# Transposes of r and k in row tiles of 64 rows, and 48 instead of 64 weight columns in the small products of an RWKV-5 and tanh-shrink kernel

## The chip, the core and the metric

The kernel runs on one core of one Trainium2 chip. The metric is the device time of one execution in microseconds. Before the change it was 600.45 us, the median of three runs (600.21 to 601.79).

## The reference

Two blocks follow each other. The first is a linear recurrence with a state of 48 x 48 for each of 4 batches and 8 heads, over 768 steps. The second is a dense block with a nonlinearity, 3072 tokens, 384 to 2048 to 384:

```python
for t in range(S):                       # B, H, S, D = 4, 8, 768, 48
    cur = einsum('bhd,bhe->bhde', u * k[:, :, t], v[:, :, t])
    y[:, :, t] = einsum('bhd,bhde->bhe', r[:, :, t], state + cur)
    state = w[..., None] * state + einsum('bhd,bhe->bhde', k[:, :, t], v[:, :, t])
x = y.transpose(0, 2, 1, 3).reshape(B * S, H * D)
h = x @ w_in
out = (h - tanh(h)) @ w_out
```

All of it is in fp32.

## The kernel before

**Units.** The recurrence is computed in 24 units. A unit takes 64 steps (`SHORT`) of two batches: its tiles have 128 partitions, the halves z = 0 and 1 being the two batches, and hold 8 heads of 48 values, each padded to 64 (`PAD`); the pads of r, of the decayed k (`kw`), of v and of the states are zero. Unit n is chunk `ch = n // 2` of batch pair `n % 2`. Heads come in four pairs p, with i = 0 and 1 in a pair.

**Steps of a unit**, in the function `unit` (from line 723):

- `fetch` (line 747) loads r, k and v with two DMAs each on SP's queue.
- `turn` (line 762) transposes r, and then k or `kw`, on TensorE: four transposes of 128 x 128, one for each pair of heads, so that heads lie on partitions and the 2 x 64 steps on columns. r goes into one PSUM bank of a two-bank tile and k into the other. This tile is `x_banks` for the first 16 units and `yk_ps` for the last 8 (`two`).
- `scale_r` (line 766) multiplies r by the powers of the decay on DVE into `rT`; `scale_k` (DVE, first two units) or `copy_k` (ACT, line 775) brings k into `kT`.
- `from_state` (line 808) multiplies the state by `rT` into `y_ps`, 16 small products. `levels` (line 819) makes the 64 x 64 blocks of k times r; DVE copies what lies above the diagonal into `at` (line 918), and ACT writes the diagonal (line 789) from the sums of r k u.
- `outputs` (line 831) adds v times `at` to `y_ps`, and `to_state` (line 845) makes the new part of the state in `kv_ps`; both are 16 products, which the trace shows as 32 instructions, as each is issued in two parts. All small products go through `put` (line 718) as tiles of 64 x 64 of the array, four of them apart in rows and columns. `to_state` is made for 22 units; the last chunk needs none.
- `to_xt` and `to_rest` (ACT, lines 864 and 869) copy `y_ps` into the dense block's input, POOL's queue moves the remaining rows (`fill`, line 874), and `keep` (line 879) adds the new part to the state.

**Dense block.** Class `Dense`: `h` (line 168) multiplies by w_in, ACT makes the tanh and helping terms, DVE joins them, and `o` (line 206) multiplies by w_out. From the ninth of 16 column blocks on and for the last token blocks the second product uses seven products in place of eight (`products`, line 257). Weights arrive as 64-bit floats and are converted on DVE and ACT (lines 137 to 143), up to about 210 us.

**What sets the order.** Nothing runs in the order of the source. `add` gives each step its engine, a planned cost, the steps that it follows and, for TensorE, the number of instructions. `Plan.order` (line 450) simulates all engines' queues with these costs and searches for a good order with some 3000 random tries; the result is each engine's fixed order. Where it leaves TensorE idle in the opening part it places filling products (line 654). Any change of a cost or a number of steps in lines 889 to 932 can so move every queue.

Of the kernel before, what the change touches and what calls it, by code (L numbers as in the profile page):

```python
# [11 lines left out]
F32 = mybir.dt.float32  # L12
# [4 lines left out]
ALU = mybir.AluOpType  # L17
# [14 lines left out]
C = 128  # L32
PAD = 64
# [267 lines left out]
class Plan:  # L301
# [214 lines left out]
def near(ctx, tc, r, k, v, w, u, out, shared, moe_w_in, moe_w_out):  # L516
# [12 lines left out]
    ps_a = ctx.enter_context(tc.tile_pool(name="n_ps_a", bufs=1, space=PSUM))  # L529
# [12 lines left out]
    HALF = [slice(z * SHORT, (z + 1) * SHORT) for z in range(2)]  # L542


    rows = fixed("rows", [2 * NP, 2, PAD])
    V.memset(rows, 1.0)
    same = fixed("same", [128, SHORT])
# [3 lines left out]
    V.memset(by[:, :, 0:1], 0.0)  # L551
    V.memset(plus, 0.0)
    V.memset(plus[:, :, 0:1], 1.0)

    def padded(name, count, new=fixed):

# [20 lines left out]
    before = before.bitcast(I32)[:, None, None, :].to_broadcast([128, 2, NP, SHORT])  # L577


    yk_ps = ps_a.tile([128, 2, 512], F32, name="yk_ps", tag="yk_ps")  # L580
    banks_now = [ExitStack(), ExitStack()]

    def banks(at, name, shapes):
# [34 lines left out]
    y_ps = yk_ps[:, :, :256].rearrange("e z (p t) -> e z p t", p=NP)  # L618
    kv_ps = yk_ps[:, :, 256 : 256 + NP * D].rearrange("d z (p e) -> d z p e", p=NP)
# [6 lines left out]
    w_up = fixed("w_up", [128, NP, 2, SHORT])  # L626
# [25 lines left out]
    def fills(to):  # L652
        def run(n):
# [6 lines left out]
    now = [add(e, 1.25 if e == "ACT" else .87, lambda e=e, at=at, x=x: e_of[e].dma_start(out=rows[at : at + NP, :, :D], in_=x.rearrange("(p i) d -> p i d", i=2)), due=-1, data=.05)  # L660
           for e, at, x in (("SP", 0, w), ("ACT", NP, u))]
# [16 lines left out]
    now = add("POOL", 1.0, bounds, [keeps])  # L678
    now = add("PE", .2, lambda: T.matmul(tab[0:1, 0:1], ok[:, 0, :1], shared["one"], start=True, stop=True), [now, downs])
# [20 lines left out]
    for n in range(weights.count):  # L700
# [14 lines left out]
    def flat4(t):  # L715
        return t.rearrange("d p z t -> d (p z t)")

    def put(*args, **how):
        T.matmul(*args, skip_group_check=True, **how)  # L719

# [2 lines left out]
    def unit(n):  # L723
# [3 lines left out]
        ch, half = divmod(n, 2)  # L727
        j, slot = divmod(n, L)
        steps_at = slice(ch * SHORT, (ch + 1) * SHORT)
        t = SimpleNamespace(at=ats[n % 2])  # L730
        rt, vt, kw, state = rts[n % (AHEAD + 1)], vts[n % (AHEAD + 1)], kws[n % 2], states[half]
        two = n >= L * (FIRST + 2)
        pair = yk_ps if two else x_banks[n == 1]
        sign = -1.0 if slot and j in dense.negative else 1.0
        r_ps, k_ps = (pair[:, i] for i in range(2))
        lev, own_lev = (pair[:, :, at : at + 256].rearrange("s i (p t) -> s i p t", p=NP) for at in ((256, 0) if two else (0, 256)))
        none = SimpleNamespace(**{x: None for x in "r k v turn rT kw kT rk du own diag state lev cp out xt rest add decay".split()})
        b1, b2, b3 = (units[n - i] if n >= i else none for i in (1, 2, 3))
# [22 lines left out]

        def turn(src, to):
            for p in range(NP):
                T.transpose(to[:, p * C : (p + 1) * C], src[:, 2 * p : 2 * p + 2, :].rearrange("t h d -> t (h d)"), ident)  # L764

        def scale_r():
            t.rT = work.tile([128, NP, 2, SHORT], F32, name="rT", tag="rT")
            V.tensor_tensor(flat4(t.rT), r_ps, flat4(w_up), ALU.mult)  # L768

        def scale_k():  # L770
            t.kT = work.tile([128, NP, 2, SHORT], F32, name="kT", tag="kT")
            V.tensor_tensor(t.kT, k_ps.rearrange("d (p z t) -> d p z t", p=NP, z=2),
                            inverse[:, :, None, 1:].to_broadcast([128, NP, 2, SHORT]), ALU.mult)

        def copy_k():
            t.kT = work.tile([128, NP, 2, SHORT], F32, name="kT", tag="kT")
            A.copy(flat4(t.kT), k_ps)

        def own():
            t.rk = work.tile([128, H, D], F32, name="rk", tag="rk")  # L780
# [18 lines left out]
                    for i in range(2):  # L799
                        put(own_lev[HALF[z], i, p], t.kU[HEAD[i], p, z], t.rT[HEAD[i], p, z], start=True, stop=True)  # L800

        def to(i, z):


            i = i ^ z if swap else i
            return slice(i * PAD, (i + 1) * PAD)

        def from_state():
            for p in range(NP if ch else 0):
                for z in range(2):  # L810
                    for i in range(2):
                        put(y_ps[to(i, z), z, p], state[HEAD[i], z, p], t.rT[HEAD[i], p, z],
                            start=p == 0, stop=False)

        def between():
# [13 lines left out]
            G.tensor_copy(extra[slot][:, :, :, D:], vt[:, 2 * NK :, :D].rearrange("s i (k x) -> s i k x", k=NK))  # L829

        def outputs():
            for p in range(NP - direct):
                for i in range(2):
                    for z in range(2):
                        put(y_ps[to(i, z), z, p], vt[HALF[z], 2 * p + i], t.at[HALF[z], i, p],
                            start=p == 0 and not ch, stop=p == NP - 1)
            for p in range(NK if direct else 0):
                for i in range(2):
                    for z in range(2):
                        put(y_ps[to(i, z), z, p], extra[slot][HALF[z], i, p], t.at[HALF[z], i, NK],  # L840
                            start=False, stop=p == NK - 1)
            if not direct:
                to_state()

        def to_state():
            for p in range(NP if more else 0):
                for i in range(2):
                    for z in range(2):
                        put(kv_ps[i * PAD : (i + 1) * PAD, z, p], kw[HALF[z], 2 * p + i], vt[HALF[z], 2 * p + i, :D],
                            start=p == 0 or not two, stop=True)  # L850

        def given(out, y):
# [36 lines left out]
        free = [b1.cp, b1.diag] if n > 2 else [units[0].cp, units[0].diag] if n == 2 else []  # L889
        if two:  # L890
            free = [b1.xt, b1.rest, b1.add, b1.cp, b1.diag]
        x.turn = add("PE", .46, lambda: turn(rt, r_ps), [x.r] + free, steps=8)
        x.kw = add("DVE", .47, lambda: V.tensor_tensor(kw[:, :, :D], t.kt[:, :, :D], w_down, ALU.mult), [x.k, downs, b2.out])
        x.turn_k = x.rk = add("PE", .46, lambda: turn(t.kt if direct else kw, k_ps), [x.k if direct else x.kw] + free, steps=8)
        both = [x.turn, x.turn_k]
        x.rT = add("DVE", .62, scale_r, both + [ups])
        if direct:
# [4 lines left out]
        if product:  # L902
            now = add("ACT", 1.05, own_k, [x.kT, w_us])
            x.own = add("PE", .7, own_levels, [now, x.rT, b2.out], steps=64)
            x.diag = add("DVE", .64, lambda: V.copy_predicated(t.at, same.bitcast(I32)[:, None, None, :].to_broadcast([128, 2, NP, SHORT]), own_lev), [x.own, b2.out])
        else:
            x.rk = add("DVE", .47, own, [x.r, x.k, b2.du, b1.rk if not b1.own else None])
            now = add("DVE", .47, lambda: V.tensor_tensor(t.rk, t.rk, ub, ALU.mult), [x.rk, bonus])
# [9 lines left out]
        x.cp = add("DVE", .64, lambda: V.copy_predicated(t.at, before, lev), [x.lev, b2.out] + ([] if product else [x.diag]))  # L918
# [105 lines left out]
    now, done = 22.0, 0  # L1024
# [335 lines left out]
```

## Time and profile before

| what | value |
|---|---|
| median of three runs | 600.45 us (600.21 to 601.79) |
| the profiled execution | 599.5 us |
| its span | 597.7 us |
| granted TensorE clock | 0.999 |
| TensorE products (PE), busy | 579.0 us, 5589 instructions |
| TensorE weight loads (PEld), busy | 491.5 us, 5589 instructions |
| DVE, ACT, POOL, busy | 465.6, 403.0, 203.7 us |
| transposes of r and k, line 764 | 29.6 us busy, 192 instructions |
| small products, line 719 | 63.6 us busy, 3008 instructions |
| DMA | 33.77 MB, 53 GB/s of HBM over the span |

The table is from the page of the profile, the rows of lines 764 and 719 from the groups by line and form. PE is a product and PEld the load of its stationary side; a load can lie under the product before it. A product's row lasts until its last result is written, and the next begins before that, so that busy times of products overlap and the distance from start to start is the cost of one. "Idle before" is the time for which an engine did nothing ahead of an instruction, and the name after the arrow is what ended it. A tile's name in a row stands for all its buffers: x_ps and yk_ps are the PSUM tiles for r and k, lev, y and the new states.

### The profile page before, as it was taken

To read this page: it belongs to the slowest core of one execution; us is meant where nothing else is said; L and a number is where in the kernel's file an instruction comes from. 1 tells how busy PE (TensorE), PEld (TensorE's weight loads), DVE (VectorE), ACT (ScalarE), POOL (GpSimd) and SP (SyncE) were. 2 spreads that over 40 slices of the span, in tenths; PEclk is the share of its full clock that TensorE was granted. 3 is DMA by queue.
4 is the path that set the end of the run, shared out by engine and by line. 5 is a ranking of instruction groups with operands and counts; after the bars stand their busy time and mean duration, and the time that the engine had idled before them with its cause. 6 is when DMAs were issued, how large, how long until landed. Compare 5 with 4: busy or idle time off the path is not lost.

```text
span 597.7 us, 14262 instructions
## 1 busy us (share of the span) xinstructions
PE 579.0 (97%) x5589; PEld 491.5 (82%) x5589; DVE 465.6 (78%) x781; ACT 403.0 (67%) x902; POOL 203.7 (34%) x366
## 2 busy tenths in 40 slices
PE   8879999999999999999999999999999999999996
PEld 5557677777777779899999999989889888999995
DVE  5799979999999999986777775665776775555765
ACT  3798798899668867766555563765675866556552
POOL 5002212201000324454555463442435354334620
PEclk9999999999999999999999999999999999999999
DMA  6976986935211311201110011120211200100101
GB/s 127 228 132 121 168 195 110 142 94 114 60 53 27 62 29 24 50 5 24 28 26 13 16 28 34 34 47 15 55 22 27 42 1 9 27 2 7 27 3 31
DMA packets 86325, 33.77 MB, mean 56 GB/s; under 512 B 78536, under 2 KB 80680, under 8 KB 86248
## 3 DMA queue, kind: packets, MB, share of 16 engines
q1 hardware_dynamic: 81084, 25.57, 22.0%
q0 software_dynamic: 4992, 6.99, 5.5%
q8 instruction: 46, 0.75, 0.6%
q14 instruction: 31, 0.25, 0.1%
q10 hardware_dynamic: 172, 0.20, 0.1%
HBM read 26.94 MB, written 4.72 MB: 53 GB/s over the span
## 4 chain that ended last, share of the span: by engine, by line
PE 72%; DVE 14%; ACT 5%; issue 4%; DMA 3%; SPq 2%; DVEq 0%; POOL 0%; ACTq 0%; POOLq 0%
PE h L168 34%; PE p L257 25%; PE o L206 5%; PE yk_ps L719 5%; SPq L752 2%; DVE tg L196 2%; DVE tg L194 1%; DVE g L192 1%; DVE g L198 1%; DMA vt<-in_v_dram 1%; PE yk_ps L764 1%; ACT at L789 1%; DMA kt<-in_k_dram 1%; DVE rT L768 1%; DVE mixed L266 1%
## 5 line engine op out<-in xcount | busy, mean ns | idle before, releaser
L168 PE MATMUL h<-xt,w_in_sb 128*128 128x256 f32 x1152 | 281.1, 381 | 1.9 <-DVE w_in_sb L143 0.9
L168 PEld LDWEIGHTS h<-xt,w_in_sb 128*128 128x128 f32 x1152 | 212.5, 190 | 32.7 <-DVE g L192 1.4
L242 POOL TENSOR_TENSOR sg<-g 128x256 f32<-128x256 f32 x69 | 53.1, 770 | 171.4 <-DVE g L198 105.3
L194 DVE SCALAR_TENSOR_TENSOR tg<-s,tg 128x512 f32<-128x512 f32 x96 | 69.5, 723 | 53.5 <-ACT tg L181 28.6
L257 PE MATMUL p<-mixed,sg 128*128 128x192 f32 x426 | 104.0, 326 | 0.0
L181 ACT ACTIVATE tg<-h 128x512 f32<-128x512 f32 x96 | 57.2, 596 | 55.7 <-PE h L168 55.7
L192 DVE TENSOR_TENSOR g<-h,th 128x512 f32<-128x512 f32 x96 | 66.0, 688 | 26.8 <-ACT tg L181 10.6
L177 ACT ACTIVATE s<-h 128x512 f32<-128x512 f32 x96 | 57.4, 598 | 41.4 <-PE h L168 41.3
L876 POOL DMA_DIRECT2D xt<-rest x66 | 32.3, 495 | 142.7 <-ACT rest L855 142.7
L179 ACT ACTIVATE th<-h 128x512 f32<-128x512 f32 x96 | 57.4, 598 | 33.4 <-PE h L168 33.2
L198 DVE COPY_PREDICATED g<-small,tg 128x512 f32<-128x512 int32 x96 | 75.6, 787 | 4.0
L196 DVE SCALAR_TENSOR_TENSOR tg<-q,tg 128x512 f32<-128x512 f32 x96 | 68.2, 711 | 9.8 <-ACT q L183 7.4
L257 PEld LDWEIGHTS p<-mixed,sg 128*128 128x128 f32 x426 | 75.0, 190 | 0.0
L206 PE MATMUL o<-w_out_sb,g 128*128 128x384 f32 x192 | 69.8, 490 | 1.7 <-DVE g L198 1.6
L257 PE MATMUL p<-w_out_sb,g 128*128 128x192 f32 x284 | 71.2, 332 | 0.0
L183 ACT ACTIVATE q<-s,m1b 128x512 f32<-128x512 f32 x96 | 69.7, 726 | 0.7
L185 ACT ACTIVATE small<-s,smallb 128x512 f32<-128x512 f32 x96 | 69.4, 723 | 0.3
L257 PEld LDWEIGHTS p<-w_out_sb,g 128*128 128x128 f32 x284 | 51.8, 190 | 7.1 <-DVE o L285 0.2
L789 ACT ACTIVATE at<-same,du 128x64 f32<-128x64 f32 x184 | 47.7, 342 | 5.3 <-DVE du L785 5.0
L206 PEld LDWEIGHTS o<-w_out_sb,g 128*128 128x128 f32 x192 | 35.5, 190 | 18.4 <-issue 1.9
L244 POOL TENSOR_TENSOR sg<-sg,g 128x128 f32<-128x128 f32 x69 | 43.2, 626 | 5.1
L246 POOL TENSOR_TENSOR sg<-sg,g 128x128 f32<-128x128 f32 x69 | 36.9, 534 | 5.1
(132 smaller groups left out, 688.2 us busy)
## 6 DMA issues: line engine op xcount, KB each, us to landing
st<-in_moe_w_out_dram SPq DMA_DIRECT2D x8, 768.0 KB, 5.0
rt<-in_r_dram SPq DMA_DIRECT2D x48, 96.0 KB, 2.9
vt<-in_v_dram SPq DMA_DIRECT2D x48, 96.0 KB, 3.5
st<-in_moe_w_in_dram SPq DMA_DIRECT2D x16, 288.0 KB, 5.4
kt<-in_k_dram SPq DMA_DIRECT2D x44, 96.0 KB, 3.4
out_dram<-o POOLq DMA_DIRECT2D x44, 96.0 KB, 2.1
st<-in_moe_w_in_dram POOLq DMA_DIRECT2D x16, 96.0 KB, 4.8
xt<-rest POOLq DMA_DIRECT2D x66, 16.0 KB, 2.2
```

Source lines behind the costliest of these rows:

```text
L168: self.nc.tensor.matmul(t.h2[:, z], self.w_in_sb[:, t.f // 2, kk, z * 128 : (z + 1) * 128], self.xts[t.j][:, kk].rearrange("p b t -> p (b ...
L177: A.activation(out, t.h, AF.Square)
L179: A.activation(out, t.h, AF.Tanh)
L181: A.activation(out, t.h, AF.Tanh, scale=G1)
L183: A.activation(out, t.s, AF.Square, bias=self.m1b)
L185: A.activation(out, t.s, AF.Relu, bias=self.smallb, scale=-1.0)
L192: V.tensor_tensor(t.g, t.h, t.th, ALU.subtract)
L194: V.scalar_tensor_tensor(t.tg, t.s, C4, t.tg, ALU.mult, ALU.mult)
L196: V.scalar_tensor_tensor(t.tg, t.q, K1, t.tg, ALU.add, ALU.mult)
L198: V.copy_predicated(t.g, t.small.bitcast(I32), t.tg)
L206: self.nc.tensor.matmul(self.outs[i], t.g2[:, z, i * C : (i + 1) * C], self.w_out_sb[:, t.f + z, :], start=t.first and z == 0, stop=t.last ...
L257: self.nc.tensor.matmul(ps[bank][:, half * n : (half + 1) * n], a, b, start=t.first and half == 0, stop=t.last, skip_group_check=True)
```

## The change

`turn` makes eight transposes in place of four: each takes the 64 rows of one half z and 128 columns, against a 64 x 64 corner of the identity, and writes 64 columns. Half 0 goes to the first PSUM bank and half 1 to the second, both for r (columns 0 to 255) and for k (columns 256 to 511). The three readers follow with another index order. In `from_state`, `outputs` (not for the first two units) and `to_state` the stationary side has 48 columns in place of 64, so that 48 partitions are written and not 64. Since `y_ps` is read in all its partitions, `yk_ps` is set to zero once at the start, on DVE. The planned costs and numbers of instructions are changed, and with them the searched order. The core of the diff:

```diff
+    V.memset(yk_ps, 0.0)
...
-        r_ps, k_ps = (pair[:, i] for i in range(2))
+        r_ps, k_ps = (pair[:, :, at : at + 256].rearrange("d z (p t) -> d z p t", p=NP) for at in (0, 256))
...
         def turn(src, to):
             for p in range(NP):
-                T.transpose(to[:, p * C : (p + 1) * C], src[:, 2 * p : 2 * p + 2, :].rearrange("t h d -> t (h d)"), ident)
+                for z in range(2):
+                    T.transpose(to[:, z, p], src[HALF[z], 2 * p : 2 * p + 2, :].rearrange("t h d -> t (h d)"), ident[HALF[z], HALF[z]])
...
-            V.tensor_tensor(flat4(t.rT), r_ps, flat4(w_up), ALU.mult)
+            V.tensor_tensor(t.rT, r_ps.rearrange("d z p t -> d p z t"), w_up, ALU.mult)
...
-            A.copy(flat4(t.kT), k_ps)
+            A.copy(t.kT, k_ps.rearrange("d z p t -> d p z t"))
...
-        def to(i, z):
+        def to(i, z, n=PAD):
...
-            return slice(i * PAD, (i + 1) * PAD)
+            return slice(i * PAD, i * PAD + n)
...
-                        put(y_ps[to(i, z), z, p], state[HEAD[i], z, p], t.rT[HEAD[i], p, z],
+                        put(y_ps[to(i, z, D), z, p], state[HEAD[i], z, p, :D], t.rT[HEAD[i], p, z],
...
-                        put(y_ps[to(i, z), z, p], vt[HALF[z], 2 * p + i], t.at[HALF[z], i, p],
+                        put(y_ps[to(i, z, n), z, p], vt[HALF[z], 2 * p + i, :n], t.at[HALF[z], i, p],
...
-                        put(kv_ps[i * PAD : (i + 1) * PAD, z, p], kw[HALF[z], 2 * p + i], vt[HALF[z], 2 * p + i, :D],
+                        put(kv_ps[HEAD[i], z, p], kw[HALF[z], 2 * p + i, :D], vt[HALF[z], 2 * p + i, :D],
...
-        x.turn = add("PE", .46, lambda: turn(rt, r_ps), [x.r] + free, steps=8)
+        turns, turned = .46, 16
+        x.turn = add("PE", turns, lambda: turn(rt, r_ps), [x.r] + free, steps=turned)
...
-            now = add("PE", .68, from_state, both + [x.rT, b1.xt, b1.rest, b1.add, b2.decay, x.kT], steps=64)
+            now = add("PE", .66, from_state, both + [x.rT, b1.xt, b1.rest, b1.add, b2.decay, x.kT], steps=64)
...
-        x.lev = add("PE", .7 if two else (1.35 if swap else 1.75) if ch else .7, levels,
+        x.lev = add("PE", .7 if two else (1.33 if swap else 1.73) if ch else .7, levels,
...
-        x.out = now = add("PE", .95 if direct else 1.3, outputs,
+        x.out = now = add("PE", .95 if direct else 1.21, outputs,
...
-            now = x.out = add("PE", .6, to_state, [now, x.kw], steps=64)
+            now = x.out = add("PE", .55, to_state, [now, x.kw], steps=64)
```

More of the change, by code (lines that the diff above doesn't have):

```diff
@@ L542, in near @@
     HALF = [slice(z * SHORT, (z + 1) * SHORT) for z in range(2)]
+    yk_ps = ps_a.tile([128, 2, 512], F32, name="yk_ps", tag="yk_ps")
     rows = fixed("rows", [2 * NP, 2, PAD])
@@ L577, in near @@
     before = before.bitcast(I32)[:, None, None, :].to_broadcast([128, 2, NP, SHORT])
-    yk_ps = ps_a.tile([128, 2, 512], F32, name="yk_ps", tag="yk_ps")
     banks_now = [ExitStack(), ExitStack()]
@@ L712, in near @@
         converted += now
-    def flat4(t):
-        return t.rearrange("d p z t -> d (p z t)")
     def put(*args, **how):
@@ L763, in turn @@
             for p in range(NP):
-                T.transpose(to[:, p * C : (p + 1) * C], src[:, 2 * p : 2 * p + 2, :].rearrange("t h d -> t (h d)"), ident)
+                for z in range(2):
+                    T.transpose(to[:, z, p], src[HALF[z], 2 * p : 2 * p + 2, :].rearrange("t h d -> t (h d)"), ident[HALF[z], HALF[z]])
         def scale_r():
             t.rT = work.tile([128, NP, 2, SHORT], F32, name="rT", tag="rT")
-            V.tensor_tensor(flat4(t.rT), r_ps, flat4(w_up), ALU.mult)
+            V.tensor_tensor(t.rT, r_ps.rearrange("d z p t -> d p z t"), w_up, ALU.mult)
         def scale_k():
             t.kT = work.tile([128, NP, 2, SHORT], F32, name="kT", tag="kT")
-            V.tensor_tensor(t.kT, k_ps.rearrange("d (p z t) -> d p z t", p=NP, z=2),
+            V.tensor_tensor(t.kT, k_ps.rearrange("d z p t -> d p z t"),
                             inverse[:, :, None, 1:].to_broadcast([128, NP, 2, SHORT]), ALU.mult)
@@ L831, in outputs @@
         def outputs():
+            n = PAD if direct else D
             for p in range(NP - direct):
@@ L891, in unit @@
             free = [b1.xt, b1.rest, b1.add, b1.cp, b1.diag]
-        x.turn = add("PE", .46, lambda: turn(rt, r_ps), [x.r] + free, steps=8)
+        turns, turned = .46, 16
+        x.turn = add("PE", turns, lambda: turn(rt, r_ps), [x.r] + free, steps=turned)
         x.kw = add("DVE", .47, lambda: V.tensor_tensor(kw[:, :, :D], t.kt[:, :, :D], w_down, ALU.mult), [x.k, downs, b2.out])
-        x.turn_k = x.rk = add("PE", .46, lambda: turn(t.kt if direct else kw, k_ps), [x.k if direct else x.kw] + free, steps=8)
+        x.turn_k = x.rk = add("PE", turns, lambda: turn(t.kt if direct else kw, k_ps), [x.k if direct else x.kw] + free, steps=turned)
         both = [x.turn, x.turn_k]
```

## The prediction

> **What bounds the kernel now.** I read the page's busy shares first, then the busy time of each engine by stretch, and then the order of TensorE's work around one unit of the recurrence.
>
> ```profile
> PE 579.0 (97%) x5589; PEld 491.5 (82%) x5589; DVE 465.6 (78%) x781; ACT 403.0 (67%) x902; POOL 203.7 (34%) x366
> ```
>
> TensorE is busy 97% of the span. By stretch (columns: stretch, its length, then busy us of PE, PEld, DVE, ACT, POOL):
>
> ```profile
> 0.00:106.00 106.00, 95.60 (x1778) 68.88 (x1782) 88.93 (x162) 80.96 (x229) 24.23 (x67) 1.00 0.82 155
> 106.00:225.00 119.00, 116.88 (x991) 87.56 (x986) 117.06 (x190) 95.62 (x195) 15.33 (x27) 1.00 0.34 71
> 225.00:355.00 130.00, 129.09 (x717) 119.98 (x708) 103.53 (x175) 80.97 (x160) 67.90 (x108) 1.00 0.11 24
> 355.00:537.00 182.00, 181.38 (x1842) 163.95 (x1841) 118.03 (x193) 112.53 (x259) 75.59 (x130) 1.00 0.13 26
> ```
>
> From 106 us on TensorE runs without a break, so there any microsecond of its work is a microsecond of the span. Before 106 us it has gaps, DVE and the DMAs (share 0.82) are as full, and the chain of waits over 0 to 106 us gives the small products (line 719, tile yk_ps) 8.5% and the transposes (line 764, tile x_ps) 3.5%: 12.7 us of that stretch. By then TensorE has spent about 47 us on all that is not dense work (my sum by the prices below), so a microsecond saved there is worth about a quarter (12.7/47).
>
> The prices come from TensorE's order of work (start, length, instructions; a group's true cost is from its start to the next start, since the ends overlap):
>
> ```profile
> 181.88 0.60 PE L764 MATMUL x_ps<-ident,kw 128*128 128x128 f32 x4
> 182.41 0.69 PE L719 MATMUL yk_ps<-at,vt 64*64 64x64 f32 x32
> 182.93 0.63 PE L719 MATMUL yk_ps<-vt,kw 64*64 64x48 f32 x32
> 183.49 1.56 PE L206 MATMUL o<-w_out_sb,g 128*128 128x384 f32 x4
> 184.88 1.46 PE L168 MATMUL h<-xt,w_in_sb 128*128 128x256 f32 x6
> 186.18 0.60 PE L764 MATMUL x_ps<-ident,rt 128*128 128x128 f32 x4
> 186.62 1.46 PE L168 MATMUL h<-xt,w_in_sb 128*128 128x256 f32 x6
> 187.91 1.45 PE L206 MATMUL o<-w_out_sb,g 128*128 128x384 f32 x4
> 189.30 0.69 PE L719 MATMUL yk_ps<-rT,state 48*64 48x64 f32 x32
> ```
>
> A turn (four transposes) between dense products takes 186.18 to 186.62, 0.44 us: 4 x 0.109, no boundary cost. Ahead of 64x64 products it takes 0.53: 0.09 is lost between the two shapes. The four o products take 1.29 elsewhere, but 1.39 when 64x64 products follow (187.91 to 189.30) and again 1.39 just after them (183.49 to 184.88). There the wait is doubled: in the single records the last small product starts 0.149 before the first o product, 0.058 of it its own turn, 0.091 idle, and then 0.104 of the next start is an unhidden weight load. So a change of array shape costs 0.09 us, and 0.055 (a transpose's load) to 0.104 (a dense load) more.
>
> **What the Trainium skill says.** "TensorEngine Tiling (Array Packing)", Key Properties: changing the tiling mode drains TensorE, and different tiles load weights and multiply in parallel. The trace agrees on both: 0.09 us at each change above, and line 719's four tiles start 7 ns apart with a new set of four each 58 ns. The same page, Gotcha 1: row tiles must not write one PSUM bank together; the change does put the halves into two banks. "TensorE: Matmul & The Clock Gate", LDWEIGHTS: a load costs its columns over 1.2 GHz, whatever the rows. The trace agrees for ordinary loads, not for transposes:
>
> ```profile
> L168 PEld LDWEIGHTS h<-xt,w_in_sb 128*128 128x128 f32 x1152 | 212.5, 190 | 32.7 <-DVE g L192 1.4 <-PE x_ps L764 1.1 <-PE x_ps L719 0.3
> L719 PEld LDWEIGHTS yk_ps<-rT,state 48*64 48x64 f32 x704 | 12.3, 134 | 12.4 <-DVE state L882 5.7 <-issue 2.7 <-DVE rT L768 1.5
> L764 PEld LDWEIGHTS x_ps<-ident,rt 128*128 128x128 f32 x64 | 7.4, 142 | 3.9 <-DVE at L918 1.8 <-issue 1.2
> ```
>
> 128 columns take 56 ns longer than 64 (190 against 134), but a transpose's 128 columns load in 142; two of line 649's loads start 61 ns apart. "PSUM — Partial Sum Buffer", bank collisions: two engines must not use one bank at once. After the change both r and k lie in both banks, so the DVE that scales r and the ACT that copies k can't overlap. They do not now either (columns: waits in all us, times, longest):
>
> ```profile
> ACT kT L777 <- DVE rT L768: 5.2, 6, 2.3
> DVE rT L768 <- ACT kT L777: 2.0, 5, 0.9
> ```
>
> **The change part by part.**
>
> (1) Transposes, inside. 48 turns of 4 x 0.109 = 0.436 become 4 pairs of 64-row tiles. If a pair runs side by side, its period is the longer of a transpose load (0.061 by line 649) and 64 moving columns (0.058, line 719); I take 0.058, 0.233 a turn. 48 x (0.233 - 0.436) = -9.7 us. Upper bound: pairs that don't overlap, or that lose the fast load, 0.109 to 0.122 a pair, 0.44 to 0.49 a turn: +9.8 to +12.3 on this term.
>
> (2) Transposes, boundaries. The 64x128 shape is new, so every edge to dense work now changes shape. In the changed program's order the 48 turns form 39 runs: 27 follow dense work, 12 small products; 37 are followed by dense work, 2 by small products. Cost: 27 x (0.091 + 0.055) + 37 x (0.091 + 0.104) + 2 x 0.091 + 12 x 0.055 = 3.9 + 7.2 + 0.2 + 0.7 = 12.0 us. The old order pays 5 x 0.093 (turn to products) and 12 x 0.055 = 1.1, and 2 more exits from small products to dense (0.2). Net +10.7. A turn alone between dense work thus goes from 0.44 to about 0.58; two back to back fall from 0.87 to 0.83. No row of before shows an edge between 128x128 and 64x128 at full clock; the lower bound is no drain, 64 x 0.091 = 5.8 us less. I take the drain, for the reason above.
>
> (3) New states (line 849). Both sides are now 48 columns. The order shows a set of four at 58 ns where 64 columns load and, once, at 45 ns where the load was already done and 48 move. 8 sets x 0.0134 = 0.107; 22 units have this step: -2.35 us. Lower gain: none, if the load has a floor of 64.
>
> (4) Outputs and reads of the state. Weights have 48 columns, but 64 still move, so the period stays 58 ns; only the first two loads, exposed, are shorter: 2 x 0.013. 22 + 22 groups: about -1.1, at least 0.
>
> (5) Evacuations. rT (0.69 us) and kT (0.58) now read two banks with a four-index pattern. Line 772 already reads with one and takes 0.69 as line 768 does; I take zero (bound +0.06 each, 2.9 us over 48, on DVE and ACT, felt only before 225 us).
>
> (6) The memset of yk_ps on DVE. 1024 columns by the row "plus" (260 columns, 0.28) is 1.1 us, from 2.15 to about 3.3; DVE is idle until 5.74 and the first product into that tile starts at 5.23, so it is hidden. Without that cover it costs 1.1.
>
> (7) Instruction stream: 192 transposes and loads more, 384 on 11,178, some 1.6 of the 46 packets of the instruction queue. Taken as zero; a fetch that TensorE waits for costs up to 2 us each.
>
> (8) Plan. The order is searched anew with changed costs, so all queues are rearranged, SP's loads and POOL's stores among them. My own sum of TensorE's work before is 565.1 us in a span of 597.7: 32.6 idle, some 20 of it before 106 us. One tenth of this more or less is 3 us.
>
> Sum over all: -9.7 + 10.7 - 2.35 - 1.1 = -2.4 us of TensorE work. Split at the output step of the twelfth unit (105.7 us): -3.0 before it, where turns lie in pairs or by small products; +0.5 after it, where most turns stand alone in dense work. On the span: 0.25 x -3.0 + 0.5 = -0.25. The profiled execution took 599.5 us with span 597.7 (1.8 outside); the median is 600.45, 0.95 above it. Carried to the median: 600.2.
>
> **Rivals.** *A, forecast: 600.2, no measurable change* (about 0.3%, 1.8 us, is what a measurement of this kernel can tell), own range 598.7 to 602.2. *B, the early saving counts in full*: 600.45 + 0.5 - 3.0 = 598.0, and lower if edges of the row shape don't drain (-5.8) or the plan is luckier. For it: TensorE is busy 90% before 106 us. Against: DVE and DMA are as full and the chain is theirs. *C, the new plan wastes a tenth more idle time*: 603.5. For it: DVE is at 98% from 106 to 225 us, so a later DVE step has no slack. *D, the pairs of row tiles don't run side by side*: place, line 764; price 0.49 a turn instead of 0.23; it decides for slower once a pair costs over about 0.074 (0.016 x (88 pairs + 104 x 0.4) = 2.1 us). The late 22 turns lose 22 x 0.25 = 5.5 in full, the early 26 lose 6.5 at a quarter to the half: 600.2 + 5.5 + 2.4 = 608. Against it: line 719's row tiles do overlap now, and the fast load stood in the one 8-row transpose (177 ns at the slow opening clock, 187 for a 128-row one). That the change does nothing is excluded: a quarter of the states' columns leaves the program.
>
> **How the numbers follow.** A 0.40, B 0.25, C 0.20, D 0.15. Faster by over 0.3% is B, 0.25; within 0.3% is A, 0.40; slower is C and D, 0.35. The range takes in C and most of B and D: 596.5 to 608.5.
>
> **What would show it.** Right: transposes of 64 rows starting 7 ns apart and sets 58 ns apart, a lone turn at 0.58, o after it at about 1.39; yk_ps<-vt,kw at 0.45 instead of 0.56 to the next start; TensorE's work about 2 us less. Wrong: single transposes 60 ns apart or more (D), a dense group after a turn at 1.29 (no drain, B), or more idle on TensorE ahead of 225 us (C).

## The result, and the profile after

The changed kernel takes 606.27 us (median of six runs, 605.43 to 608.19) beside 600.76 for the kernel before on the same chip (600.21 to 601.82): ratio 1.0093, 95% interval 1.0074 to 1.0112. It is 5.5 us slower. The profiled execution took 607.26 us, its span 605.5. From the page of the kernel after: busy shares, the clock that TensorE was granted in 40 slices (9 is full), and the instruction queue.

```profile
PE 582.4 (96%) x5781; PEld 485.7 (80%) x5781; DVE 466.4 (77%) x782; ACT 403.3 (67%) x902; POOL 201.0 (33%) x366
...
PEclk9889899999999999999999999999999999999999
...
q8 instruction: 47, 0.77, 0.5%
```

The clock was below full speed in three of the first five slices, up to 76 us; before, all 40 digits were 9. By stretch (length, busy us of PE, PEld, DVE, ACT, POOL, then granted clock, DMA share, GB/s):

```profile
0.00:106.00 106.00, 91.53 (x1696) 62.84 (x1697) 86.91 (x155) 75.79 (x216) 24.89 (x68) 0.94 0.72 144
106.00:225.00 119.00, 116.37 (x1107) 84.71 (x1108) 115.43 (x191) 92.97 (x196) 12.32 (x24) 1.00 0.40 80
...
355.00:537.00 182.00, 181.89 (x1847) 160.56 (x1846) 120.93 (x198) 117.56 (x272) 75.55 (x131) 1.00 0.13 27
```

Only the first stretch is worse: TensorE did 82 instructions fewer there, DVE 2.0 us less work, ACT 5.2 less, and the clock was 0.94. The twelfth unit's output step, at 105.7 us before, starts at 118.7 now, with 3.9 us more dense work done by then: 9.1 us are lost. What follows it takes 486.8 us instead of 492.0; of these 5.2 us, 3.9 are the dense work already done, and 1.3 are gained. So the loss lies in the opening.

The operations themselves, from TensorE's order of work after (start, length, instructions):

```profile
118.69 0.67 PE L717 MATMUL yk_ps<-at,vt 64*48 64x64 f32 x32 [0.27 <-DVE at L919]
119.17 0.54 PE L717 MATMUL yk_ps<-vt,kw 64*48 64x48 f32 x32
119.64 1.56 PE L206 MATMUL o<-w_out_sb,g 128*128 128x384 f32 x4
...
362.48 1.46 PE L168 MATMUL h<-xt,w_in_sb 128*128 128x256 f32 x6
363.87 0.46 PE L763 MATMUL yk_ps<-ident,kw 64*128 64x64 f32 x8
364.26 1.56 PE L168 MATMUL h<-xt,w_in_sb 128*128 128x256 f32 x6
365.66 0.49 PE L257 MATMUL p<-w_out_sb,g 128*128 128x192 f32 x2
```

New states go from 0.56 to 0.47 us (119.17 to 119.64), outputs from 0.52 to 0.48. The lone turn takes 0.39, and the dense groups on both sides of it are longer by about 0.1 each (362.48 to 363.87 is 1.39 and 364.26 to 365.66 is 1.40, where six h products took 1.29 from 186.62 to 187.91 before): 0.60 in all. In the single records two transposes of a pair start 3 to 4 ns apart and pairs 61 to 64 ns apart, except that the second pair of most turns starts 110 to 115 ns after the first. The weight loads by form, and the two waits between the readers of r and k, of the kernel after:

```profile
L763 PEld LDWEIGHTS x_ps<-ident,rt 64*128 64x128 f32 x128 | 5.4, 143 | 2.7 <-issue 1.6 <-DVE at L919 0.5
L717 PEld LDWEIGHTS yk_ps<-rT,state 48*48 48x48 f32 x704 | 11.7, 123 | 12.4 <-DVE state L882 4.3 <-DVE rT L767 2.9 <-issue 2.8
```

```profile
ACT kT L776 <- DVE rT L767: 5.4, 6, 2.5
DVE rT L767 <- ACT kT L776: 2.5, 5, 1.1
```

The 64-row load of a transpose is as fast as the whole one was (143 against 142 ns), and sharing two banks changed those waits by 0.2 and 0.5 us. So much was about as priced. What was not priced stands in two places. The first, at 17 us (a bracket is idle time and what ended it; "issue" means that the profile shows nothing that was waited for):

```profile
16.86 0.56 PE L717 MATMUL x_ps<-rT,kT 48*64 48x64 f32 x20 [0.45 <-DVE kT L771]
18.14 0.45 PE L717 MATMUL x_ps<-rT,kT 48*64 48x64 f32 x12 [0.72 <-issue]
...
21.43 0.58 PE L717 MATMUL yk_ps<-at,vt 64*64 64x64 f32 x24 [1.78 <-DVE at L919]
```

One step of 32 products stops after 20 of them for 0.94 us, start to start, though it waits for no other engine. The second place, at 54 to 66 us:

```profile
50.71 0.67 PE L717 MATMUL yk_ps<-rT,state 48*48 48x64 f32 x32
...
54.73 0.70 PE L168 MATMUL h<-xt,w_in_sb 128*128 128x256 f32 x2
56.98 0.67 PE L168 MATMUL h<-xt,w_in_sb 128*128 128x256 f32 x2 [1.55 <-DMA xt<-rest]
58.84 0.67 PE L168 MATMUL h<-xt,w_in_sb 128*128 128x256 f32 x2 [1.19 <-DMA xt<-rest]
59.44 1.10 PE L717 MATMUL yk_ps<-rT,state 48*48 48x64 f32 x32
60.33 1.07 PE L717 MATMUL x_ps<-rT,kT 48*64 48x64 f32 x32
...
64.19 1.11 PE L717 MATMUL yk_ps<-at,vt 64*48 64x64 f32 x32
```

TensorE waits twice for a tile from DMA, and then all its work takes twice as long: 0.89 us for 32 products (59.44 to 60.33) instead of 0.48. The granted clock was 0.5 from 59.4 to 66.2 us, and also at 21.9 to 25.3 and 38.9 to 42.4 us.

### The profile page after: what moved, and what is told of

The parts are those of the page before. It is cut to its first block, busy times and chain, and to the rows that moved or that the text cites. A ratio compares the mean times of both kernels' runs of the same rounds, so it can differ in the third digit from the quotient of the medians.

```text
span 605.5 us, 14670 instructions
## 1 busy us (share of the span) xinstructions
PE 582.4 (96%) x5781; PEld 485.7 (80%) x5781; DVE 466.4 (77%) x782; ACT 403.3 (67%) x902; POOL 201.0 (33%) x366
## 4 chain that ended last, share of the span: by engine, by line
PE 76%; DVE 6%; DMA 5%; ACT 4%; issue 4%; SPq 3%; POOL 1%; DVEq 0%; ACTq 0%; POOLq 0%
PE h L168 37%; PE p L257 26%; PE o L206 6%; PE yk_ps L717 4%; SPq L750 3%; DMA st<-in_moe_w_in_dram 2%; DMA xt<-rest 1%; PE yk_ps L763 1%; POOL xt L876 1%; DMA st<-in_moe_w_out_dram 1%; DVE rT L767 1%; DVE at L919 1%; ACT s L177 1%; DVE tg L194 1%; DVE g L198 1%
## 5 line engine op out<-in xcount | busy, mean ns | idle before, releaser
L168 PE MATMUL h<-xt,w_in_sb 128*128 128x256 f32 x1152 | 285.7, 385 | 2.7 <-DMA xt<-rest 2.7
L194 DVE SCALAR_TENSOR_TENSOR tg<-s,tg 128x512 f32<-128x512 f32 x96 | 71.1, 741 | 36.6 <-ACT tg L181 20.0
L181 ACT ACTIVATE tg<-h 128x512 f32<-128x512 f32 x96 | 57.2, 596 | 58.5 <-PE h L168 56.9
L198 DVE COPY_PREDICATED g<-small,tg 128x512 f32<-128x512 int32 x96 | 71.1, 741 | 4.7 <-DVE tg L196 0.5
L206 PE MATMUL o<-w_out_sb,g 128*128 128x384 f32 x192 | 71.3, 495 | 0.1
L246 POOL TENSOR_TENSOR sg<-sg,g 128x128 f32<-128x128 f32 x69 | 41.0, 594 | 5.1
L244 POOL TENSOR_TENSOR sg<-sg,g 128x128 f32<-128x128 f32 x69 | 36.6, 530 | 5.2
```

The source lines that it names most:

```text
L168: self.nc.tensor.matmul(t.h2[:, z], self.w_in_sb[:, t.f // 2, kk, z * 128 : (z + 1) * 128], self.xts[t.j][:, kk].rearrange("p b t -> p (b ...
L181: A.activation(out, t.h, AF.Tanh, scale=G1)
L194: V.scalar_tensor_tensor(t.tg, t.s, C4, t.tg, ALU.mult, ALU.mult)
L198: V.copy_predicated(t.g, t.small.bitcast(I32), t.tg)
L206: self.nc.tensor.matmul(self.outs[i], t.g2[:, z, i * C : (i + 1) * C], self.w_out_sb[:, t.f + z, :], start=t.first and z == 0, stop=t.last ...
```

## Experiments

The planner fixes each queue's order from planned costs and instruction counts alone, so that the operations and the order can be exchanged. In what follows an *entry* is one load or one product in TensorE's stream, counted from its start: an ordinary float32 product counts four (the trace has two loads and two products for each), a transpose two. A *break* is a hole inside a run of small products that waits for no other engine.

**Operations and order apart.** First, the changed operations with the planned costs of the kernel before, and so its order:

```diff
-        turns, turned = .46, 16
+        turns, turned = .46, 8
...
-        x.out = now = add("PE", .95 if direct else 1.21, outputs,
+        x.out = now = add("PE", .95 if direct else 1.3, outputs,
```

> All operations of the change, but the planned costs and instruction counts of before, so that every queue keeps the order of before. Theory 'order' (the 5.5 us come from the rearranged queues in the opening 120 us, not from the operations): TensorE's own work falls by 2.0 us (2.75 less up to the twelfth unit's outputs, 0.7 more after), so 599 to 601.5. Theory 'operations' (array-shape drains and shorter bursts cost TensorE more than priced, or make it lose its clock): 604 to 607, with granted clock near 0.99 as after the change.

Second, the reverse: the operations of before, with the planned costs of the change.

```diff
-        x.turn = add("PE", .46, lambda: turn(rt, r_ps), [x.r] + free, steps=8)
+        x.turn = add("PE", .46, lambda: turn(rt, r_ps), [x.r] + free, steps=16)
...
-        x.out = now = add("PE", .95 if direct else 1.3, outputs,
+        x.out = now = add("PE", .95 if direct else 1.21, outputs,
```

> The operations of before, with the planned costs and instruction counts of the change, so that the queues stand in the changed order. Theory 'order': the opening's waits and the lost clock come with the order, so 605 to 609 and a granted clock near 0.99. Theory 'operations': 600 to 602, clock 0.999.

Third and fourth, each half of the change alone, in the old order: row tiles with 64 columns of weights as before,

```diff
-                        put(kv_ps[HEAD[i], z, p], kw[HALF[z], 2 * p + i, :D], vt[HALF[z], 2 * p + i, :D],
+                        put(kv_ps[i * PAD : (i + 1) * PAD, z, p], kw[HALF[z], 2 * p + i], vt[HALF[z], 2 * p + i, :D],
```

> The row tiles of the transposes alone (64 weight columns kept), in the order of before. By the sum of the prices TensorE's work is 1.4 us longer (1.0 less early, 2.5 more late). Theory 'order': 601 to 603.5. Theory 'operations': 604 or more.

and 48 columns of weights with the transposes whole as before.

```diff
-                for z in range(2):
-                    T.transpose(to[:, z, p], src[HALF[z], 2 * p : 2 * p + 2, :].rearrange("t h d -> t (h d)"), ident[HALF[z], HALF[z]])
+                T.transpose(to[:, p * C : (p + 1) * C], src[:, 2 * p : 2 * p + 2, :].rearrange("t h d -> t (h d)"), ident)
```

> The 48 weight columns alone (transposes of before kept), in the order of before. By the sum of the prices TensorE's work is 3.5 us shorter, half of it late. Theory 'order': 597 to 599, the fastest of the four. Theory 'operations': at or above 600.8, if the 48 columns bring no gain on the chip.

| kernel | us, median (range) | ratio to before, 95% | TensorE's work by the prediction's prices, against before |
|---|---|---|---|
| new operations, old order | 603.59 (601.82 to 608.1) | 1.0056 [1.0030, 1.0082] | |
| old operations, new order | 602.38 (601.57 to 603.38) | 1.0036 [1.0023, 1.0049] | 0 |
| row tiles alone, old order | 604.79 (601.68 to 605.18) | 1.0062 [1.0045, 1.0079] | +1.4 |
| 48 columns alone, old order | 599.46 (598.64 to 600.82) | 0.9978 [0.9971, 0.9984] | -3.5 |

Before took 600.71 beside these. The last column was worked out ahead of the runs and is no measurement; the busy time of TensorE's products on the pages agrees with it, 580.6 us in row tiles alone and 575.6 in 48 columns alone against 579.0 before. The first two kernels lie between what either theory had said: the order and the operations both cost something. The new order alone costs 1.7 us. The 48 columns alone gain 1.25 of 3.5 us of work, and this kernel beats both of the study. Row tiles lose 4.1 us in the old order, with or without the 48 columns (604.79 against 600.71, 603.59 against 599.46), where their work is only 1.4 more. The traces show where. TensorE's order in the new operations in the old order (this trace is of an execution of 607.35 us, one of the two slowest of seven, so that its first break is no typical one):

```profile
17.26 0.56 PE L717 MATMUL x_ps<-rT,kT 48*64 48x64 f32 x20
21.95 0.69 PE L717 MATMUL x_ps<-rT,kT 48*64 48x64 f32 x12 [4.12 <-issue]
```

In row tiles alone:

```profile
17.07 0.56 PE L717 MATMUL x_ps<-rT,kT 48*64 48x64 f32 x20 [0.47 <-DVE kT L771]
19.14 0.45 PE L717 MATMUL x_ps<-rT,kT 48*64 48x64 f32 x12 [1.51 <-issue]
...
22.29 0.58 PE L717 MATMUL yk_ps<-at,vt 64*64 64x64 f32 x24
...
75.71 0.67 PE L717 MATMUL yk_ps<-at,vt 64*64 64x64 f32 x26
77.86 0.28 PE L717 MATMUL yk_ps<-at,vt 64*64 64x64 f32 x3 [1.48 <-issue]
```

Before reaches the same outputs, in the same order, 1.99 us earlier:

```profile
20.30 0.58 PE L719 MATMUL yk_ps<-at,vt 64*64 64x64 f32 x24
```

Step by step against before, row tiles alone fall behind by 1.7 us more at the break at 77.9 us. The granted clock of this execution (604.73 us) was full up to 602 us, so that the loss needs no half clock.

Counted in entries the breaks lie at 442, 950 and 2474 in row tiles alone, at 442 and 2474 in the new operations in the old order, at 442 after; the distances, 508 and 1524, are 2 and 6 times 254. None of before, the old operations in the new order and 48 columns alone has a break. In before, entry 442 lies among the filling products after that run, 950 is the first filler after a turn, and 2474 is the first entry of the products with `state`. The reading from here on: TensorE's stream comes in packets with edges at 188 + 254 m, and an edge close behind a burst of short entries makes TensorE wait for the next packet.

The traces settle this reading, since they record every packet of the instruction queue q8 (16,384 bytes each; 46 before, 47 after). Packet m belongs to the edge at 188 + 254 m:

| kernel | edge | its packet, start to end, us | the entry at the edge starts at |
|---|---|---|---|
| after | 442 | 15.17 to 16.69 | 18.14, after a break |
| new operations, old order | 442 | 19.08 to 20.55 | 21.95, after a break |
| row tiles alone | 442 | 15.74 to 17.38 | 19.14, after a break |
| row tiles alone | 2474 | 74.86 to 76.43 | 77.86, after a break |
| before | 442 | 15.04 to 16.50 | 19.35, no break |

In the 16 traces of this study there are 24 holes of TensorE of over 0.09 us at such an edge (counted up to 12 entries early) for which the profile shows no other engine. In each of them TensorE goes on 1.2 to 1.8 us after the end of that edge's packet; at the other 674 edges the packet had ended at least 1.36 us ahead. Three holes of this kind, of 0.1 to 0.5 us, lie elsewhere. So a break is the wait for a packet. Its length follows from when the packet starts: in the 24 cases 2.1 to 7.3 us after TensorE passed the edge before, and after 225 us, where the DMAs are little used, never more than 1.7 us after. What delays a packet in the opening wasn't tried.

At 54 to 58 us the old operations in the new order meet the same wait for DMA, shorter and without the half clock:

```profile
55.55 0.67 PE L168 MATMUL h<-xt,w_in_sb 128*128 128x256 f32 x2 [0.72 <-DMA xt<-rest]
56.15 0.69 PE L719 MATMUL yk_ps<-rT,state 48*64 48x64 f32 x32
```

**Two repairs that failed.** Was it the half clock? Filling products ahead of three waits were to hold the clock up:

```diff
+    more = {units[1].outs.n: (3, idle), units[3].turn_k.n: (6, x_banks[1][:, 0])}
     for t in plan.order():
+        count, to = more.get(getattr(t, "n", None), (0, None))
+        for _ in range(count):
+            fills(to)[0][1]()
...
-        for kk in range(d.NK):
+        busy = t.j == 1 and t.f == 0 and z == 0
+        for kk in (0, 0, 0, 0, 1, 0, 1, 2) if busy else range(d.NK):
```

> The changed kernel in its own order, with TensorE kept busy at three waits of the opening: three more filling products ahead of the outputs of unit 1 (wait at 19 to 21 us), six ahead of the transposes of k of unit 3 (wait at 36 to 39 us), and five more products of the same h chain while its inputs land (55 to 59 us; the last chain is complete, so the values are those of before). No wait is taken away. Theory 'clock' (most of the loss is TensorE at half its clock after these waits): granted clock back to 0.996 or more, 602 to 604. Theory 'order alone' (the waits themselves are the loss): 606 to 608, since the added products bring nothing.

It took 612.03 us (608.6 to 616.21; ratio 1.0187, 1.0154 to 1.022). The first two groups did keep the clock at 1.0 from 16 to 52 us, but the products with the state at 50.71 us in the kernel after start 0.7 us later here, not earlier: half clock at 22 and 39 us had cost little. The third group waited for DMA too, ran at half clock and stood on the path, and a new break of 2.4 us came at 119 us (entry 3744):

```profile
58.50 5.77 PE L169 MATMUL h<-xt,w_in_sb 128*128 128x256 f32 x16 [2.97 <-DMA xt<-rest]
```

Was it that one wait for the tile? The first h of the third tile was put behind the products of the state:

```diff
+    order = plan.order()
+    order.remove(tiles[2].h0)
+    order.insert(order.index(units[5].lev) + 1, tiles[2].h0)
```

> The changed kernel with one step of TensorE's order moved: the first half of h of the third tile, which stood at 54.7 us and waited for its input's last rows until 58.8 us, now stands behind the state and level products of the same unit. No work is added or left out. If the late rows and the half clock after them are a large part of the loss: 602.5 to 604. If the loss lies in the instruction stream or is spread over the whole order: 605.5 to 607.

It took 608.9 (605.27 to 609.91; ratio 1.0117, 1.0089 to 1.0145): missed. No trace of it was kept, so it isn't known whether the wait went away; moving that one step did not help.

**Other draws of the order.** The search starts from a random seed, 5 in both kernels. Seeds 6 and 7 (`chance = Random(6)`):

> The kernel before with another seed of the order search (6 in place of 5), so another drawn order of the same operations; TensorE's work by the prices 567.0 us (565.1 before). If the draw of the order is worth some us by itself: anywhere in 601 to 607. If the order before was an ordinary one: 600 to 602.5.

> The changed kernel with seed 6; TensorE's work by the prices 562.4 us (562.7 in the change). If the draw makes the difference: a value apart from 606.3 by 2 us or more, 600 to 605 as likely as more. If the operations themselves cost it (instruction fetch, clock): 605 to 608 again.

> The changed kernel with seed 7; TensorE's work by the prices 562.5 us. As with seed 6: apart from 606.3 by 2 us or more if the draw decides, 605 to 608 if the operations do.

> The kernel before, with its order of work searched from seed 7 instead of 5; the change with that seed took 607.3 and with seed 6 603.7, the kernel before with seed 6 603.2. Theory that the draw of the order makes most of the loss: 603 to 606 here too. Theory that the row tiles make it, by their place in the stream and the half clock that follows: 600.5 to 603, 4 us or more below the change with this seed.

| seed | before | change | breaks of the change (start to start) |
|---|---|---|---|
| 5 | 600.76 | 606.27 | 0.94 |
| 6 | 603.21 (601.73 to 604.03) | 603.69 (602.45 to 604.79) | 4.8, 0.8, 2.7 |
| 7 | 603.17 (601.99 to 605.04) | 607.33 (606.3 to 608.86) | 4.0, 1.8, 0.7 |

The kernel before had the better draw with seed 5 by 2.4 us. With seed 7 the change loses 4.2 more; the run at 17 us breaks at the same entry again, while before meets the same edge among fillers. (Before with seed 7, without row tiles, also has a break of 0.47 us inside a run of small products, at entry 690.) The change with seed 7, then before with seed 7:

```profile
16.51 0.56 PE L717 MATMUL x_ps<-rT,kT 48*64 48x64 f32 x20
20.88 0.69 PE L717 MATMUL x_ps<-rT,kT 48*64 48x64 f32 x12 [3.81 <-issue]
```

```profile
17.82 1.98 PE L654 MATMUL h<-ident 128*128 128x512 f32 x4
21.61 1.45 PE L654 MATMUL h<-ident 128*128 128x512 f32 x4 [1.81 <-issue]
```

With seed 6 the longest break costs nothing measurable. The change and before with seed 6 reach the same step together:

```profile
22.56 0.70 PE L717 MATMUL x_ps<-rT,kT 48*64 48x64 f32 x15 [4.61 <-issue]
...
30.63 0.34 PE L717 MATMUL yk_ps<-rT,state 48*48 48x64 f32 x8
```

```profile
21.86 0.66 PE L764 MATMUL x_ps<-ident,kw 128*128 128x128 f32 x4 [1.79 <-DVE kw L893]
...
30.72 0.70 PE L719 MATMUL yk_ps<-rT,state 48*64 48x64 f32 x32
```

So a break's length is not always its price: later waits can swallow it.

**The stream shifted by additions.** Eight or twelve products of 8 columns among the first fillers put 32 or 48 entries ahead of all else:

```diff
+            for _ in range(more.pop(0) if more else 0):
+                T.matmul(to[:, :8], ident, ident[:, :8], start=True, stop=True)
```

> The new operations in the old order, with twelve products of 8 columns added among the first fillers, ahead of 5 us where TensorE has no work: 48 more entries (loads and products counted) stand ahead of everything else. Theory of the stream: breaks come at fixed entry numbers (442, 950, 2474), so the one that stood in the middle of x_ps<-rT,kT now falls on what was entry 394, in the fillers before that run, where TensorE waits for kT anyway; the run of 32 pieces goes through in 0.5 us at about 17 us, and the time falls from 603.6 to between 601 and 602.5. Rival (the row-tile operations themselves, or the run's own place, cause the break): the break stays after 20 of 32 pieces of x_ps<-rT,kT near 17.4 us, and the time stays 603 to 604.

> 48 columns alone in the old order, the fastest so far (599.5), with eight products of 8 columns added among the first fillers: 32 more entries. Theory of the stream: entry 442 now falls on what was entry 410, after 20 of the 32 pieces of x_ps<-rT,kT near 17 us, the place where the kernels with row tiles break; a break of 0.3 to 4 us comes there although this kernel has no row tiles, and the time is 600.3 to 602.5. Rival (row tiles cause the breaks): no break, and 599.2 to 599.8 as without the shift.

> The changed kernel with the same twelve added products. Theory of the stream: its one break, 0.94 us at entry 442, falls into the fillers before the run and is gone; later edges move too. The first 54 us then run about 1 us earlier, and the time is 604.5 to 605.8 if nothing else moves, since most of the loss lies at 54 to 66 us, where TensorE waits for the third tile and then runs at half clock. Rival: the break stays, and the time is 606 as before.

The times are no test: 613.84 (610.92 to 619.64), 604.71 (604.04 to 605.4) and 614.48 (610.54 to 616.85). The added products stand in the first microseconds, where all products are slow (two fillers of 512 columns take 2.01 us at 5.43 us in the new operations in the old order, 1.06 at 7.95), and delayed the first turn by 3.9 us in the second kernel, and the first product into `yk_ps` by 5.1 and 5.3 us in the others. The places are a test. 48 columns alone, shifted by 32, has no row tiles and now breaks in the run at 21 us, after 19 of 32 products (entry 440):

```profile
21.14 0.56 PE L724 MATMUL x_ps<-rT,kT 48*64 48x64 f32 x19
23.01 0.45 PE L724 MATMUL x_ps<-rT,kT 48*64 48x64 f32 x13 [1.31 <-issue]
```

In the new operations shifted by 48 that run is whole, and the hole lies before the fillers, where entry 442 now is:

```profile
20.50 0.57 PE L721 MATMUL yk_ps<-vt,kw 64*48 64x48 f32 x32
25.34 2.72 PE L659 MATMUL h<-ident 128*128 128x512 f32 x4 [4.26 <-issue]
27.99 1.13 PE L721 MATMUL x_ps<-rT,kT 48*64 48x64 f32 x32
```

The place in the stream makes the break, not the row tile.

**The stream shifted by leaving the first ten turns whole.** This adds no entries:

```diff
+        whole = n < 5
...
+                if whole:
+                    T.transpose(to[:, :, p], src[:, 2 * p : 2 * p + 2, :].rearrange("t h d -> t (h d)"), ident)
-                for z in range(2):
+                for z in range(0 if whole else 2):
```

> The new operations in the old order, but the first five units (ten turns) transposed whole as in the kernel before: 80 entries fewer, at no more work (a lone turn priced 0.44 against 0.58, a pair 0.87 against 0.83). Entry 442 falls on what was 474, in the fillers after x_ps<-rT,kT, ahead of a wait of some 3 us; entry 2474 falls on what was 2554, in dense products. Theory of the stream: no break inside x_ps<-rT,kT at 17.4 us, less or no half clock after it, and 603.6 falls to 600.0 to 601.8, leaving about what the pricing of the row tiles gives over 48 columns alone (599.5 + 1.4). Rival (the row tiles lose by something else than the opening's stream): 603 to 604.5.

> The changed kernel with the same first five units transposed whole. Theory of the stream: its break of 0.94 us at entry 442 goes, later edges fall elsewhere; what is left is the redrawn order, which cost 1.7 with the old operations (602.4): 602 to 604.5 against 606.3. Rival (the wait for the third tile at 54 to 66 us and the half clock come with this order whatever the stream): 605.5 to 607.

Measured: 601.59 (600.83 to 603.73; ratio 1.0016, 1.0009 to 1.0023) instead of 603.59, and 602.71 (600.89 to 607.02; ratio 1.0034, 1.0019 to 1.0048) instead of 606.27; before took 600.86. Both lie where the stream's theory put them. The exchange isn't of the place alone, since the ten turns are other operations too (a lone one is priced 0.14 us shorter when whole). TensorE's order in the changed kernel with ten turns whole: the run at 17 us is unbroken, and at 57 us there is one wait and no half clock.

```profile
16.70 0.70 PE L717 MATMUL x_ps<-rT,kT 48*64 48x64 f32 x32
...
50.42 0.66 PE L717 MATMUL yk_ps<-rT,state 48*48 48x64 f32 x32
...
56.85 0.67 PE L168 MATMUL h<-xt,w_in_sb 128*128 128x256 f32 x2 [1.27 <-DMA xt<-rest]
57.45 0.67 PE L717 MATMUL yk_ps<-rT,state 48*48 48x64 f32 x32
57.94 0.65 PE L717 MATMUL x_ps<-rT,kT 48*64 48x64 f32 x32
...
60.01 0.66 PE L717 MATMUL yk_ps<-at,vt 64*48 64x64 f32 x32
```

All ten turns are done by 50 us, and there the two kernels are only 0.3 us apart (50.71 and 50.42). The same step of outputs starts at 64.19 in the kernel after and at 60.01 here. The stretch from 62 to 64 us in the kernel after, then here (DVE is the third number; the clock the third from the end):

```profile
62.00:64.00 2.00, 2.00 (x6) 1.26 (x4) 1.75 (x4) 0.00 (x0) 0.00 (x0) 0.50 0.01 1
```

```profile
62.00:64.00 2.00, 2.00 (x9) 1.55 (x9) 1.06 (x2) 1.50 (x5) 0.00 (x0) 1.00 0.87 128
```

At half clock six products fill the 2 us; ACT has nothing to do, the DMAs stand still (share 0.01 against 0.87), and only DVE still works, up to 64 us. Each kernel with ten whole turns has one break left in the opening: in the old order 1.58 us at entry 2468, in the changed order 1.91 us at entry 3486 (107.5 us).

## Why the prediction was wrong

It said 600.2 and no measurable change; the kernel lost 5.5 us. The runs divide this into three parts that add up to 5.6: the redrawn order, 602.38 - 600.71 = 1.7; the operations in it with the first ten turns whole, 602.71 - 602.38 = 0.3; the ten early row-tile turns, 606.27 - 602.71 = 3.6. Each difference is good to about 1 us.

Steps (1) to (6) held in the main. (1) and (2): pairs run side by side, at 61 to 64 ns where 58 were priced (the step named a load of 61 ns as the longer time and then took the shorter one, about 0.6 us over all), each edge of shape costs its drain, a lone turn 0.60 where 0.58 were priced. In row tiles alone TensorE's products are busy for 1.6 us more, where +1.0 was worked out. This agrees with "TensorEngine Tiling (Array Packing)" of the Trainium skill, Key Properties, as the prediction used it. (3) and (4): with 48 columns alone they are busy for 3.4 us less, where 3.45 were worked out (2.35 + 1.1). (5): rT takes 685 ns (690 before), kT 589 (585). (6): the first product into `yk_ps` starts at 5.05 us (5.23 before), so that the memset was hidden. The weight of a quarter for early work was if anything too high: 10 of the 22 units with these steps lie before the twelfth's outputs, so that the rule gives the 48 columns 0.25 x 1.6 + 1.9 = 2.3 us, and they brought 1.25 (1.0 to 1.7). The sum of TensorE's work, -2.4 us, rests on the prices; no run measures it by itself, but its parts don't contradict it.

Step (7) failed: "Instruction stream ... Taken as zero". The 384 added entries were weighed as 1.6 more packets, when what counts is where the edges of all packets fall: eight entries more for each turn move every later edge against the program, and TensorE stops there until the packet has come. The edge at entry 442 tells it: wherever it lies 34 to 40 entries into the run at 17 or 21 us, that run breaks, with row tiles or without; where it lies among fillers, the run is whole. The bound of "up to 2 us each" was low as well: 4.6 us of idle time in one case. In the old order the price can be read directly. At the edge 2474 row tiles alone, the new operations and the kernel with ten whole turns have breaks of 1.69, 1.75 and 1.58 us, and there each falls behind the kernel with the same order and no break by 1.7 to 1.8 us more: this break is paid in full.

For the changed kernel itself the way from the ten turns to the 3.6 us is not shown. Its break of 0.94 us at 17 us is not what is paid: by 50 us only 0.3 us of it is left. The loss arises at 54 to 66 us. Two waits for DMA stand close together there, in which TensorE does little for some 3.4 us, and half clock follows. The last two of the six DMAs of xt<-rest land at 58.5 and 58.7 us, and at 54.8 and 56.7 with ten whole turns, though they are issued only 0.3 us later; in the kernel after, a load of 288 KB is issued ahead of the fifth of them (51.65 and 52.06 us), with ten whole turns behind it (51.90 and 51.78). Whether this exchange is the cause was not tried. "TensorE: Matmul & The Clock Gate" of the Trainium skill, Part 1, says that the clock falls to half after an idle window of about 3.4 us and that the window runs freely. The trace agrees with the length: half clock lasts 3.4 or 6.8 us, and its three starts (21.87, 38.94, 59.42) lie 5 and 6 times 3.41 us apart. But the 3.41 us ahead of them were not wholly idle: TensorE was busy for 1.62, 0.33 and 1.25 us of them. In the kernel after, half clock at 59 to 66 us goes with some 2 us of the loss: against it the kernel with ten whole turns is 1.99 us ahead at the read of the state (57.45 against 59.44) and 4.18 at the outputs. But half clock at 22 and 39 us, which both have, cost little, and seed 6 swallowed a break of 4.8: in the opening DVE, DMA and TensorE take turns as the bound, and no rule for the price of a break there came out of the runs.

Step (8), taken as zero too, was off by 1.7 us. Rival C had its mechanism (the new plan wastes idle time before 225 us) and priced it at 3 us; seeds 6 and 7 of the kernel before, 2.2 to 2.5 us slower, show that this is a matter of the draw and not of the change. The new order and the ten turns together, 1.7 + 3.6, are the loss; neither alone is. Rivals B and D are excluded: the early saving didn't come in full, edges of the row shape do drain, and the pairs do run side by side.

Left open: what makes a packet start late in the opening, and how the ten turns lead to the late rows at 54 us. The kernel after varies by 2.8 us from run to run. Its six runs have a mean granted clock of 0.985 to 0.994; with ten whole turns it is 0.990 to 1.0, and the three slowest of these runs (604.5 us and more) have 0.990 or 0.991. This fits a window that runs freely, but wasn't tested.

## What to carry to other kernels

When a change adds short instructions to an engine with bursts of them, count entries ahead of the bursts in the opening, look for holes at fixed entry numbers that no semaphore ends, and compare them with the packets of the instruction queue in the trace. Here leaving ten turns whole, 80 entries fewer, was worth 2.0 and 3.6 us, more than the 1.25 us of the 48 columns. Where a planner redraws the order, run the old operations in the new order first, since that difference is no property of the change. Here the 48 columns without the row tiles, in the old order, are the version to keep: 599.46 us.

## What was not expected of the hardware

- Holes in TensorE's stream at entries 442, 696, 950, 2474, 3236, 3490 and 3744 (up to 12 early), all 188 + 254 m, of 0.3 to 4.8 us start to start, mostly within or after bursts of short products. TensorE goes on 1.2 to 1.8 us after the end of a packet of 16,384 bytes of its instruction queue.
- The load of a transpose's 128 columns is as quick with 64 rows (143 ns, pairs at 61 to 64 ns) as with 128 (142 ns).
- The clock fell to half in the kernels without row tiles as well (before with seed 6 at 22.7 to 29.5 us, with seed 7 at 32.7 to 39.5 us). So the new shape isn't needed for it. In the kernel after it followed stretches of 3.41 us in which TensorE was busy for 0.33 to 1.62 us.
